# Ninety-nine shared exponential pairs, VectorE's lists taken by turns, and the last skip products on VectorE, in a kernel that mixes an SSM and an attention block

## Chip, core and metric

The kernel runs on one core of one Trainium2 chip. The metric is the device time of one execution in microseconds. Engines are called PE (matrix products), ACT (ScalarE), DVE (VectorE), POOL (GpSimd) and SP (SyncE, which here issues nearly all DMAs).

## What is computed

With x of 2048 tokens by 1024 channels (bf16), a gate g per token mixes an SSM a and an attention block b:

```python
g = sigmoid((x * gate_w).sum(-1))
h[t] = Lam_bar * h[t-1] + B_bar @ x[t]            # 1024 complex states
a = 2 * Re(C @ h) + x * Dskip
b = softmax(q k^T / sqrt(32)) v @ wo              # 32 heads of 32, q k v = x @ wqkv
out = g * a + (1 - g) * b
```

## The kernel before

**Attention in bursts.** The 32 heads are taken in 8 groups of 4 (`GROUPS`), the queries in 8 blocks of 256 (`QUNITS`), the keys in 8 blocks of 256 (`BURSTS`): 512 bursts. `burst` (from L1612) issues eight score products (L1624) into PSUM and two exponentials on ACT of 128x1024 each (L1643). `pv` (L1709) multiplies their results with V, some bursts later. After eight bursts `normalize` (L1716) takes a reciprocal and a product on DVE from PSUM's bank "O", and a transposing DMA brings the result to OT.

**Shared exponentials.** In some bursts ACT's second exponential leaves out a quarter and is 128x768 (L1640). DVE does that quarter: it copies 256 columns from PSUM to integers (`x_in`, L1633), before ACT may take the rest; two such bursts make a *pair*, on which DVE runs three polynomial steps over 512 columns (`x_q`, L1667, L1668, L1664, each reading the one before), POOL makes bf16 bits of them (L1665), and PE multiplies them with V (L1688). `X_PLAN` lists the pairs, 92 of them; `X_AT` says which bursts of eight they take. A group of four bursts in the plan holds one pair.

**Dense work between.** Each burst has room for four products of 512 columns (`MM_PER_PERIOD`), all accumulating in PSUM bank 7: chains of eight or sixteen products, whose evacuation DVE does at their end. The chains are: u = B x (`d_u`, L1457, 64 chains, 32 items with real and imaginary part), projections to Q, K and V of the next group (`d_qk` L1426, `d_v` L1445), SSM output (`d_c`, L1504, 32 tiles of 128x512 in four quarters `ch` of the sequence, each tile sixteen products in four bursts), and output products (`d_out`, L1535). A tile of SSM output also has four products of 128 columns with a diagonal matrix of Dskip (`diagD`, L1510): that is D times x. Its evacuation (L1517) multiplies by g into the single buffer `Ag`, and a DMA stores it (`ag_scratch`); the store is read back for the output products (`ld_a`, L1527).

**SSM items.** Each u goes out to DRAM and comes back by `ld_u` (L1474) into one buffer. An item's steps on DVE (`item_ops`, L1353 and the scans L1362) form the states of 512 tokens. SSM output of a quarter needs all eight items of it.

**Order.** `build` writes the order of every engine's queue by hand, burst by burst. DVE has three lists: `xbg` (steps of pairs), `bg` (steps of items) and `bg2` (tables, folding of C, and the like). At the end of each burst the planner has room up to a limit, tries how many steps of each list fit by a table of durations, and takes the best sum; steps of one list follow each other, those of pairs first. A chain's evacuation follows at its end. SP's queue is in program order: weights are loaded at the 26th and 29th burst of a group, C by `ld_c` (L1081) from burst 28 on, two transposes each four bursts, B by `ld_b` (L1076) after each evacuation of u. K and V weights have two buffers. The output weights come in five loads.

**Tail** (from L1956). Sums of the last output tiles, split into a high and a low bf16 part (`hi`, `lo`, L1553 and L1554), are put into PSUM by four products with the identity (`preload`, L1975) ahead of the last value products.

Of the kernel before, what the change touches and what calls it, by code (L numbers as in the profile page):

```python
# [922 lines left out]
GROUPS = 8  # L923
# [9 lines left out]
C_LOADS = 28  # L933

X_AT = ((0, 2), (4, 6), (0, 4))
X_PLAN = (64, 72, 80, 88, 92, 96, 100, 104, 108, 112, 116, 120, 124, 128, 132, 136, 144, 152, 160, 168, 172, 176, 180, 184, 188, 192, 200, 208, 216, 224, 228, 232, 236, 240, 244, 248, 252, 256, 260, 264, 272, 280, 288, 296, 304, 312, 316, 320, 324, 328, 332, 336, 344, 352, 356, 360, 364, 368, 372, 376, 380, 384, 388, 392, 396, 400, 404, 408, 412, 416, 420, 424, 428, 432, 436, 440, 444, 448, 452, 456, 460, 464, 468, 472, 476, 480, 484, 488, 492, 496, 500, 504)
X_COLS = 256
F_TS, F_ST = 1.32, 1.24
I_MM = 0.61
X_LAST = 0.735  # L940
# [18 lines left out]
class FastPath:  # L959

    def __init__(self, nc, S, es, d, flag):
# [11 lines left out]
        wb = T("wb", [128, 8192], BF)  # L973
        self.wq = wb[:, 0:1024].rearrange("p (a n) -> p a n", a=8)
        self.wkv = wb[:, 1024:5120].rearrange("p (s q a n) -> p s q a n", s=2, q=2, a=8)
        self.bT = wb[:, 5120:8192].rearrange("p (s a n) -> p s a n", s=3, a=8)

        row = lambda o, n: wb[:, o:o + 1024 * n].rearrange("p (a n) -> p a n", a=n)
        self.wo3 = [row(1024, 2), row(5120, 3), row(3072, 1), self.cT[0][:, 0:1, :], self.cT[0][:, 1:2, :]]
        self.wo = [(self.wo3[0][:, a, :], "wo0") for a in range(2)] + [(self.wo3[4][:, 0, :], "wo4")] + [(self.wo3[1][:, a, :], "wo1") for a in range(3)]  # L980
        self.wo += [(self.wo3[3][:, 0, :], "wo3"), (self.wo3[2][:, 0, :], "wo2")]
# [5 lines left out]
        self.hpx = wb[:, 5120:8192].rearrange("p (k n) -> p k n", k=6)  # L987
# [18 lines left out]
        self.diagD = T("diagD", [128, 8, 128], BF)  # L1006
        self.init = T("init", [128, 2, 8], F32)
# [57 lines left out]
    def w_of(self, g, part):  # L1065
        return (self.wkv[:, g % 2, part - 1], ("w", g % 2, part)) if part else (self.wq, ("w", 0, 0))
# [241 lines left out]

    def fold_ops(self, j):
# [32 lines left out]
    def item_ops(self, j, ch, n):  # L1342
# [9 lines left out]
        def tt(c, o, a, b, op, r, w):  # L1352
            ops.append((c, lambda: dve(lambda e: e.tensor_tensor(o, a, b, op), r, w)))  # L1353
# [3 lines left out]
        ops.append((0.0, lambda: self.used_u(n)))  # L1357
# [6 lines left out]
        if ch < 3:  # L1364
            ops.append((0.0, lambda: self.pool(lambda e: e.tensor_copy(self.hl[:, :, j], ht[:, :, 511]), [("ht", 0), ("ht", 1)], [("hl", j)])))
# [770 lines left out]
```

## Time and profile before

| What | Value |
|---|---|
| Runs of before | 929.36 us median of 3 (927.99 to 930.2) |
| The profiled execution | 928.11 us, of which the span on the core is 926.3 |
| PE, ACT, DVE, POOL busy | 902.5, 907.3, 758.4, 86.8 us |
| Granted PE clock, mean | 0.996 |

How to read it: a line of groups names the source line, the engine, the operation, what it writes and reads, and a count; then busy time, mean duration and idle time before. A line of the chain has start, duration and what ran; the chain is followed back from the last instruction, so what it holds set the end. A line of the timeline has start, duration and, in square brackets, idle time before it and what ended it. An answer by source line gives the shortest, median and longest duration in ns and first and last start in us. Instructions of ACT and PE overlap their neighbours, so starts, not durations, give the pace. DMAs show as their issue on SP's queue (SPq).

### The profile page before, as it was taken

How to read it: one execution, taken by the hardware profiler on the slowest of the kernel's cores; microseconds unless marked ns; L12 is line 12 of the kernel's file. 1: busy time of each engine (PE TensorE's matmuls, PEld its weight loads, DVE VectorE, ACT ScalarE, POOL GpSimd, SP SyncE). 2: the span in 40 equal slices, each digit the busy share in tenths (PEclk: the TensorE clock that was granted, in tenths of full speed). 3: DMA queues.
4: the chain of work that ended last, by engine and by line, in shares of the span. 5: the costliest groups of instructions: out<-in, count | busy, mean ns of one | idle time of the engine just before them, and what ended most of it. 6: DMA issues, size and time to landing. Idle time of an engine off the chain costs nothing.

```text
span 926.3 us, 33979 instructions
## 1 busy us (share of the span) xinstructions
PE 902.5 (97%) x15316; PEld 503.9 (54%) x15316; DVE 758.4 (82%) x1310; ACT 907.3 (98%) x1034; POOL 86.8 (9%) x156
## 2 busy tenths in 40 slices
PE   8899999999999999999999999999999999999996
PEld 4554754557555565546655565555655655445553
DVE  2788989998989999989989999899988655776665
ACT  6999999999999999999999999999999999999996
POOL 2000000111000101011111020000010010001010
PEclk9999999999999999999999999999999999999998
DMA  9569747750457101272012511413001112424312
GB/s 195 87 116 184 93 84 138 144 116 5 81 113 152 50 20 49 67 147 53 19 51 65 126 45 31 104 63 103 20 15 43 31 51 77 156 83 128 114 62 75
DMA packets 170934, 77.69 MB, mean 84 GB/s; under 512 B 147232, under 2 KB 155424, under 8 KB 170784
## 3 DMA queue, kind: packets, MB, share of 16 engines
q1 hardware_dynamic: 168624, 74.94, 36.3%
q8 instruction: 121, 1.98, 0.9%
q10 hardware_dynamic: 2160, 0.53, 0.3%
q14 instruction: 29, 0.24, 0.1%
HBM read 25.18 MB, written 20.97 MB: 50 GB/s over the span
## 4 chain that ended last, share of the span: by engine, by line
PE 52%; ACT 40%; DVE 4%; DMA 2%; SPq 1%; issue 1%; POOL 0%; DVEq 0%; ACTq 0%
ACT f_pt L1643 32%; PE f_ps L1709 14%; PE f_ps L1624 10%; PE f_ps L1426 9%; PE f_ps L1504 7%; PE f_ps L1457 6%; ACT f_pt L1640 5%; PE f_ps L1445 5%; SPq L1062 1%; ACT f_cT L1643 1%; PE f_ps L1688 1%; DMA f_xT<-in_A_x_dram 1%; ACT f_Et L1643 1%; DMA f_wb<-in_A_B_im_dram 1%; DMA f_ub<-u_scratch 0%
## 5 line engine op out<-in xcount | busy, mean ns | idle before, releaser
L1643 ACT ACTIVATE f_pt<-f_ps 128x1024 bf16<-128x1024 f32 x760 | 728.8, 1090 | 1.5 <-PE f_ps L1624 1.3
L1709 PEld LDWEIGHTS f_ps<-f_V,f_pt 128*128 128x128 bf16 x7184 | 222.2, 96 | 95.3 <-issue 68.7
L1709 PE MATMUL f_ps<-f_V,f_pt 128*128 128x33 bf16 x7184 | 258.0, 178 | 0.0
L1624 PE MATMUL f_ps<-f_Q,f_K 32*128 32x256 bf16 x4096 | 203.3, 273 | 10.8 <-ACT f_pt L1643 3.3
L1640 ACT ACTIVATE f_pt<-f_ps 128x768 bf16<-128x768 f32 x184 | 165.3, 898 | 0.7 <-PE f_ps L1624 0.6
L1624 PEld LDWEIGHTS f_ps<-f_Q,f_K 32*128 32x128 bf16 x4096 | 60.7, 92 | 148.0 <-ACT f_pt L1643 120.6
L1457 PE MATMUL f_ps<-f_xT,f_wb 128*128 128x512 bf16 x512 | 131.5, 379 | 1.6 <-DMA f_wb<-in_A_B_im_dram 0.7
L1665 POOL TENSOR_SCALAR f_xp<-f_xq 128x512 int16<-128x512 f32 x92 | 67.3, 732 | 646.0 <-DVE f_xq L1664 471.3
L1426 PE MATMUL f_ps<-f_xT,f_wb 128*128 128x512 bf16 x464 | 119.3, 379 | 0.1
L1633 DVE TENSOR_SCALAR f_xi<-f_ps 128x256 int32<-128x256 f32 x184 | 77.4, 421 | 17.6 <-PE f_ps L1624 13.3
L1362 DVE TENSOR_TENSOR_SCAN f_ht<-f_pf,f_init,f_ut 128x512 bf16<-128x512 f32 x64 | 81.3, 1279 | 0.0
L1504 PE MATMUL f_ps<-f_cT,f_hp 128*128 128x512 bf16 x272 | 74.5, 379 | 0.1
L1667 DVE SCALAR_TENSOR_TENSOR f_xq<-f_xi 128x512 f32<-128x512 uint16 x92 | 63.7, 692 | 3.2
L1668 DVE SCALAR_TENSOR_TENSOR f_xq<-f_xq,f_xi 128x512 f32<-128x512 f32 x92 | 63.6, 692 | 3.1
L1664 DVE SCALAR_TENSOR_TENSOR f_xq<-f_xi,f_xq 128x512 f32<-128x512 int16 x92 | 63.5, 690 | 2.6
L1457 PEld LDWEIGHTS f_ps<-f_xT,f_wb 128*128 128x128 bf16 x512 | 40.1, 96 | 40.5 <-issue 8.6
L1535 PE MATMUL f_ps<-f_wb,f_OT 128*128 128x512 bf16 x188 | 61.2, 381 | 0.4 <-DVE f_Et L1547 0.4
L1445 PE MATMUL f_ps<-f_wb,f_xT 128*128 128x128 bf16 x896 | 59.3, 219 | 0.0
L1426 PEld LDWEIGHTS f_ps<-f_xT,f_wb 128*128 128x128 bf16 x464 | 36.1, 96 | 35.6 <-issue 7.6
L1461 DVE CAST f_ub<-f_ps 128x512 bf16<-128x512 f32 x64 | 44.1, 688 | 10.4 <-PE f_ps L1457 9.7
L1445 PEld LDWEIGHTS f_ps<-f_wb,f_xT 128*128 128x128 bf16 x896 | 50.4, 97 | 3.8 <-issue 3.8
L1722 DVE RECIPROCAL f_rc<-f_ps 128x8 f32<-128x8 f32 x63 | 13.1, 207 | 47.6 <-PE f_ps L1688 43.5
(149 smaller groups left out, 822.5 us busy)
## 6 DMA issues: line engine op xcount, KB each, us to landing
u_scratch<-f_ub SPq DMA_DIRECT2D x64, 128.0 KB, 2.1
f_ub<-u_scratch SPq DMA_DIRECT2D x32, 256.0 KB, 3.0
ag_scratch<-f_Ag SPq DMA_DIRECT2D x32, 256.0 KB, 2.0
f_hp<-ag_scratch SPq DMA_DIRECT2D x32, 256.0 KB, 3.0
f_wb<-in_B_wqkv_dram SPq DMA_DIRECT2D x21, 256.0 KB, 4.1
out_dram<-f_xT SPq DMA_DIRECT2D x16, 256.0 KB, 2.2
f_OT<-f_On SPq DMA_TRANSPOSE x63, 2.3
f_wb<-in_B_wo_dram SPq DMA_DIRECT2D x1, 768.0 KB
```

Source lines behind the costliest of these rows:

```text
L1362: ops.append((1.24, lambda ri=ri: dve(lambda e: e.tensor_tensor_scan(ht[:, ri, :], rr, ut[:, ri, :], self.init[:, ri, j:j + 1], ALU.mult, ...
L1426: mms.append((1, lambda e, f, l, a=a, w=w: e.matmul(ps[:, bank, :], w[:, a, :], xT[:, a, 512 * ch:512 * (ch + 1)], start=f, stop=l), [tok] ...
L1445: m = e.matmul(ps[:, bank, 128 * q:128 * (q + 1)], xT[:, a, 128 * kt:128 * (kt + 1)], w[:, a, :], start=(a == 0), stop=(a == 7))
L1457: mms.append((1, lambda e, f, l, a=a: e.matmul(ps[:, 7, :], bT[:, (2 * n + ri) % 3, a, :], xT[:, a, 512 * ch:512 * (ch + 1)], start=f, sto ...
L1504: mms.append((1, lambda e, f, l, j=j, ri=ri, h=h: e.matmul(ps[:, 7, :], h[:, cols], cT[ri][:, j, 512 * cb:512 * (cb + 1)], start=f, stop=l ...
L1624: m = e.matmul(ps[:, 2 * sl[h // 2] + h % 2, 256 * kl:256 * (kl + 1)], K[32 * h:32 * h + 32, g % 2, 128 * kt:128 * (kt + 1)], Q[32 * h:32 ...
L1633: first = self.dve(lambda e: e.tensor_scalar(self.xi[:, b % 2, X_COLS * n:X_COLS * (n + 1)], ps[:, 2 * s + 1, 512 - X_COLS:512], X_A, X_LO ...
L1640: self.S.op("act", lambda e: e.activation(flat(self.tile[p]), flat(ps[:, 2 * s:2 * s + 2, :]), ACT.Exp, scale=SCALE), reads=[("S", s)], wr ...
L1643: self.act(lambda e: e.activation(self.tile[p], ps[:, 2 * s:2 * s + 2, :], ACT.Exp, scale=SCALE), [("S", s)], [("pt", p)], "exp")
L1665: self.pool(lambda e: e.tensor_scalar(bits, xq[:], X_K, 128.0 * (E0 + 126.0), ALU.mult, ALU.add), ["xq"], p2, "x_p")
L1667: return [(0.73, 0.0, lambda: self.dve(lambda e: e.scalar_tensor_tensor(xq[:], lo, E2 / E3 * w, lo, ALU.add, ALU.mult), i2, ["xq"], "x_q") ...
L1709: m = e.matmul(ps[:, 6, o:o + 33], self.tile[p][:, h2, 256 * kl + 128 * qt:256 * kl + 128 * (qt + 1)], V[:, g % 2, 2 * i + kl, h, :], star ...
```

## The change

1. **Seven more pairs**: 268, 276, 284, 292, 300, 308 and 348 are new in `X_PLAN`, 99 in all.
2. **Steps by turns**: each step now carries a duration and a surcharge `DEP` if the step before it came from the same list; `mixed` adds up a choice of steps from the three lists, changing list at every step where it can, and says from which list comes the first. Durations in the table are smaller by 0.01 to 0.12 us.
3. **D times x**: in the last quarter (`ch` 3, eight tiles, 32 bursts) the diagonal products go; x and a broadcast Dskip are loaded, DVE writes x times g times D into `Ag` (`skip`, put on `bg2`), and the evacuation adds PSUM times g to it.
4. **Loads**: K, V and Q weights have one buffer each; K and V are loaded at the first burst of a group for the next (the first time K at the 18th, V at the start), Q at the 39th. C's loads begin at burst 32. All output weights but the last load when SSM output is done.
5. **hi and lo** go on `bg2`; **preload** is split, two products ahead of the last value products and two behind.

```diff
-C_LOADS = 28
+C_LOADS = 32
+W_AT = (38, 0, 17)
-I_MM = 0.61
-X_LAST = 0.735
+DEP = 0.12
+I_MM = 0.6
+X_LAST = 0.615
...
+    def ld_skip(self, dn):
+        tt, cb = divmod(dn.tile, 2)
+        self.dma(lambda e: e.dma_start(self.xn[:, dn.k], self.x2[128 * tt:128 * (tt + 1), 512 * cb:512 * (cb + 1)]), [], [("xn", dn.k)], "ld_xn")
+
+    def skip(self, dn):
+        tt, cb = divmod(dn.tile, 2)
+        if not dn.skipped:
+            dn.skipped = True
+            self.dve(lambda e: e.scalar_tensor_tensor(self.Ag, self.xn[:, dn.k], self.gcol[:, 0, tt:tt + 1], self.Dbc[:, 512 * cb:512 * (cb + 1)], ALU.mult, ALU.mult),
+                     [("xn", dn.k), "Dbc", "g0"], ["Ag"], "skip")
...
-        for q in range(4):
+        for q in range(4 if ch < 3 else 0):
...
+                self.skip(dn)
+                self.dve(lambda e: e.scalar_tensor_tensor(a, ps[:, 7, :], self.gcol[:, 0, tt:tt + 1], a, ALU.mult, ALU.add), [("bank", 7), "g0"], [at], "evac_c")
...
-                    self.dve(lambda e: e.tensor_copy(hi, su), [("sum7", i)], [("hi", i)])
-                    self.dve(lambda e: e.tensor_tensor(lo, su, hi, ALU.subtract), [("sum7", i), ("hi", i)], [("lo", i)])
+                    self.bg2 += [(0.34, lambda: self.dve(lambda e: e.tensor_copy(hi, su), [("sum7", i)], [("hi", i)])),
+                                 (0.72, lambda: self.dve(lambda e: e.tensor_tensor(lo, su, hi, ALU.subtract), [("sum7", i), ("hi", i)], [("lo", i)]))]
...
+    def mixed(self, xs, bs, ts):
+        rest = {"x": list(xs), "b": list(bs), "t": list(ts)}
+        t, lane, lead = 0.0, self.lane, ""
+        while True:
+            some = [s for s in "xbt" if rest[s]]
+            if not some:
+                return t, lead
+            s = next((s for s in some if s != lane), some[0])
+            if rest["b"] and rest["b"][0][0] == 0.0:
+                s = "b"
+            c, d = rest[s].pop(0)
+            lead = lead or s
+            if c > 0:
+                t += c + (d if s == lane else 0.0)
+                lane = s
...
-            if pg == 25 and g + 2 < GROUPS:
-                assert g or not (proj[0] or cur and cur.tag == "proj")
-                for part in (1, 2):
-                    self.ld_w(g + 2, part)
-            if pg == 28 and g + 1 < GROUPS:
-                assert not (cur and cur.tag == "proj")
+            if pg == W_AT[1 if g else 2] and g + 1 < GROUPS:
+                self.ld_w(g + 1, 1)
+                if g:
+                    self.ld_w(g + 1, 2)
+            if pg == W_AT[0] and g + 1 < GROUPS:
+                assert not proj[0]
                 self.ld_w(g + 1, 0)
...
+                            if ch == 3:
+                                self.bg2.append((0.73, lambda dn=cur: self.skip(dn)))
+                            if cs and cs[0][0] == 3:
+                                if ch == 2:
+                                    self.dma(lambda e: e.dma_start(self.Dbc[:], self.d["A_Dskip"].unsqueeze(0).to_broadcast([128, 1024])), [], ["Dbc"], "ld_D")
+                                self.later.append((p + 2, lambda dn=cs[0][1]: self.ld_skip(dn)))
...
-                            v = (u + (0.3 * i if ended is not None else 9.0 * i) + 0.05 * sum(bs[:j]), i, j, k)
+                            v = (u + (0.3 * i if ended is not None else 9.0 * i) + 0.05 * sum(x[0] for x in bs[:j]), i, j, k, lead)
...
-        preload()
-        self.pv(4 * NBURST - 4, 4 * NBURST)
+        preload(0)
+        self.pv(4 * NBURST - 4, 4 * NBURST - 2)
+        self.pv(4 * NBURST - 2, 4 * NBURST)
+        preload(1)
```

More of the change, by code (lines that the diff above doesn't have):

```diff
@@ L1520, in evac @@
             self.c_end = self.p
-        return self.chain(mms, "c", evac)
+        dn = self.chain(mms, "c", evac)
+        dn.tile, dn.k, dn.skipped = tile, k % 2, False
+        return dn
     def ld_a(self, k):
@@ L1744, in build @@
             self.ld_b(m)
-        for part in (1, 2):
-            self.ld_w(1, part)
+        self.ld_w(1, 2)
         self.plan()
@@ L1784, in build @@
         first = FIRST
-        wo1 = wo6 = last = False
+        wo1 = last = False
         nal = nc = 0
@@ L1806, in build @@
                 if n == 1:
-                    self.xbg += [[c, wait, f] for c, wait, f in self.x_ops(b)]
+                    self.xbg += self.x_ops(b)
+                self.lane = "x"
             q0, q1 = self.quarters[p]
@@ L1838, in build @@
+            if pg == W_AT[0] and g + 1 < GROUPS:
+                assert not proj[0]
                 self.ld_w(g + 1, 0)
             wsv = self.d["B_wo"].rearrange("(a p) n -> p a n", p=128)
[L1840 to L1842 removed]
+            if not wo1 and not cs and cur is None and self.c_left[3] == 0:
```

140 lines of the change are left out of this document (71 added, 69 removed).

## The prediction

> **What bounds the kernel now.** I began with the page's first part, then asked for ScalarE's two exponentials by source line, then for the chain of work in a quiet stretch, and last for PE's timeline at a few bursts.
>
> ```profile
> PE 902.5 (97%) x15316; PEld 503.9 (54%) x15316; DVE 758.4 (82%) x1310; ACT 907.3 (98%) x1034; POOL 86.8 (9%) x156
> ...
> L1643 ACT ACTIVATE f_pt<-f_ps x760: 1018/1103/1309, 9.9 to 916.1; 128x1024 bf16<-128x1024 f32 x190
> L1640 ACT ACTIVATE f_pt<-f_ps x184: 805/908/978, 131.9 to 907.2; 128x768 bf16<-128x768 f32 x184
> ...
> 491.47 6.42 ACT f_pt L1643 x7
> 497.90 0.70 ACT f_pt L1640
> ...
> 910.69 6.60 ACT L1643 ACTIVATE f_pt<-f_ps 128x1024 bf16<-128x1024 f32 x7
> ```
>
> Two engines look full, so busy shares decide nothing. The chain does: seven full exponentials take 6.42 us, 0.917 each, and a shortened one 0.70. The recorded durations (1.10 and 0.91) are longer because neighbours overlap. The program has 512 bursts with two exponentials each: 1024, of which 184 are short. 840 x 0.917 + 184 x 0.70 = 899 us. The first starts at 9.9 (the fourth number of L1643's row) and the last ends at 910.69 + 6.60 = 917.3: 907.4 us. So ScalarE is the bound nearly everywhere, some 8 us are stalls of it, and 9 us of the span lie behind it.
>
> PE is close behind. The next rows are the first score products of bursts 264, 284, 356, 380, 402 and 434, so that differences give the pace.
>
> ```profile
> 482.09 0.29 PE L1624 MATMUL f_ps<-f_Q,f_K 32*128 32x256 bf16 x4
> 517.55 0.40 PE L1624 MATMUL f_ps<-f_Q,f_K 32*128 32x256 bf16 x8
> 644.50 0.29 PE L1624 MATMUL f_ps<-f_Q,f_K 32*128 32x256 bf16 x4
> 685.83 0.40 PE L1624 MATMUL f_ps<-f_Q,f_K 32*128 32x256 bf16 x8
> 723.93 0.40 PE L1624 MATMUL f_ps<-f_Q,f_K 32*128 32x256 bf16 x8
> 780.24 0.40 PE L1624 MATMUL f_ps<-f_Q,f_K 32*128 32x256 bf16 x8
> ```
>
> Bursts 356 to 379 run projections beside two pairs per eight bursts: 41.33 / 24 = 1.722 us each, which is ScalarE's own pace (12 x 0.917 + 4 x 0.70 = 13.80 per eight, 1.726 each). Bursts 402 to 433 also have two pairs, but run SSM output with its diagonal products: 56.31 / 32 = 1.760. There PE is the bound by 0.034. Bursts 264 to 283 run SSM output with one pair per eight: 1.773, where ScalarE needs 14.24 / 8 = 1.780.
>
> **The change, part by part.**
>
> *Seven more pairs* (of bursts 268, 276, 284, 292, 300, 308, 348). A pair shortens two exponentials by 0.217: 0.43 us, 3.0 for seven. That is only taken where PE doesn't become the bound. 268, 276 and 348 lie in SSM output with diagonal products, if its place stays: eight bursts go from 14.24 to 8 x 1.760 = 14.08, 0.16 each. 284 is half in it: 0.30. The other three take 0.43. Sum: **-2.1 us** (-3.0 if PE never binds).
>
> *Diagonal products*, four in each of the last quarter's eight tiles:
>
> ```profile
> 501.28 0.22 PE L1510 MATMUL f_ps<-f_diagD,f_xT 128*128 128x128 bf16 x1
> 501.34 0.38 PE L1504 MATMUL f_ps<-f_cT,f_OT 128*128 128x512 bf16 x1
> ```
>
> The next product starts 0.06 us behind one, so 32 are 1.9 us of PE, one per burst. ScalarE's 1.726 stops the gain: (1.760 - 1.726) x 32 = **-1.1 us**. What replaces them is VectorE's, with room there:
>
> ```profile
> 480.00:640.00 160.00, 159.02 (x2684) 87.92 (x2682) 146.70 (x236) 160.00 (x183) 18.07 (x27) 1.00 0.30 76
> 724.00:780.00 56.00, 56.00 (x928) 30.06 (x928) 31.35 (x56) 55.87 (x65) 4.94 (x8) 1.00 0.14 44
> ```
>
> The columns behind the window are PE, weight load, VectorE, ScalarE, GpSimd. VectorE is busy 31.35 of 56 us there; eight skip steps of 128x512 add 8 x 0.7 (the rows of f_xq below have that size). The evacuation still reads PSUM, with one operand more; this form isn't shown alone, and I leave it at its 0.75 (row at 744.85 below), since up to 0.3 more would still end in that idle time. The nine loads for it, with DMA engines busy 0.14 of that stretch (the column before the last), I cost at nothing; the price without cover is the rival below.
>
> *Steps by turns.* Does VectorE have time for seven pairs between 480 and 640 us? It idles 13.3 of 160.
>
> ```profile
> 504.31 0.69 DVE L1667 SCALAR_TENSOR_TENSOR f_xq<-f_xi 128x512 f32<-128x512 uint16 x1
> 505.03 0.69 DVE L1668 SCALAR_TENSOR_TENSOR f_xq<-f_xq,f_xi 128x512 f32<-128x512 f32 x1
> 505.76 0.69 DVE L1664 SCALAR_TENSOR_TENSOR f_xq<-f_xi,f_xq 128x512 f32<-128x512 int16 x1
> 506.37 1.70 DVE L1353 TENSOR_TENSOR f_ut<-f_ht,f_tq 128x512 f32<-128x512 bf16 x2
> ...
> L1667 DVE SCALAR_TENSOR_TENSOR f_xq<-f_xi x62: 691/692/693, 138.7 to 697.2; 128x512 f32<-128x512 uint16 x62
> ```
>
> A step that reads its predecessor's result starts 0.72 to 0.73 us behind it (504.31, 505.03, 505.76); one that doesn't starts after 0.61 (506.37). So a stranger between two such steps saves 0.11. A pair costs 2 x 0.42 (the copies from PSUM, row at 745.59 below) + 3 x 0.72 = 3.0 us now, seven cost 21. Saving: 62 pairs up to 700 us with three places each, 62 x 3 x 0.11 = 20 us, and the SSM items have dependent steps as well; bounds 0 and about 30. I take the middle, 15 us, since a stranger isn't always ready. With the idle time that covers the seven pairs. So the turns bring no time themselves; they pay for the pairs.
>
> The Trainium skill (VectorE: DVE Perf Modes, section "The DRAIN you can't avoid") states that the next operation starts only when the pipe is empty, whether or not a semaphore lies between, and that chained operations can't skip it. By that rule order would be worth nothing here; the 0.61 and 0.72 above don't bear it out for operations without a dependence.
>
> *Moved loads.* ScalarE's largest stall stands at burst 34:
>
> ```profile
> 66.79 1.30 SPq L1081 DMA_TRANSPOSE f_cT<-in_A_C_im_dram  x1
> 68.14 1.28 SPq L1071 DMA_DIRECT2D f_wb<-in_B_wqkv_dram  x1
> ...
> 69.53 3.79 DMA f_ub<-u_scratch
> ...
> 75.27 0.57 PE L1709 MATMUL f_ps<-f_V,f_OT 128*128 128x33 bf16 x16 [1.24 <-DVE f_On L1723]
> ...
> 77.36 1.94 ACT L1643 ACTIVATE f_OT<-f_ps 128x1024 bf16<-128x1024 f32 x2 [1.34 <-PE f_ps L1624]
> ```
>
> The load of u is issued at 69.53, behind two transposes of C and a weight load (3 x 1.3, some 3.9 us of SP's queue), lands at 73.3, VectorE waits for it with the normalization behind, PE waits for that, ScalarE for PE. The change starts the C loads at burst 32 and that weight load at 38, so u goes 3.9 us earlier: **-1.3 us** (bounds -1.4 and 0, if the next collision takes its place). Four bursts later, C is still not late: the last loads slip some 7 us, and the first step on C waits until tables are made.
>
> ```profile
> L1318 DVE TENSOR_SCALAR f_OT<-f_cT,f_pf x8: 1275/1282/1287, 135.9 to 288.8; 128x2048 f32<-128x2048 bf16 x8
> L1081 SPq DMA_TRANSPOSE f_cT<-in_A_C_im_dram x8: 1242/1299/2480, 66.8 to 115.6; - x8
> ...
> 404.64 4.86 DMA f_wb<-in_A_B_im_dram
> ...
> 401.95 1.88 SPq L1071 DMA_DIRECT2D f_wb<-in_B_wqkv_dram  x2
> ...
> 410.97 2.85 ACT L1643 ACTIVATE f_pt<-f_ps 128x1024 bf16<-128x1024 f32 x3 [0.33 <-PE f_ps L1624]
> ```
>
> At 402 the same happens to a load of B behind two weight loads: 0.4 us with its start. It goes: **-0.4**. But K and V weights now load at each group's first burst, where in three groups B and u stream as well; one such stall in three: **+0.4** (0 to 1.2). The output weights now load in one bunch; the eight bursts of Q projections between the last SSM tile and the first output product (14 us) hide them.
>
> *The split into hi and lo* is now placed by the planner instead of run at once:
>
> ```profile
> 815.13 0.44 DVE f_Et L1553
> ...
> 823.94 0.35 DVE f_xi L1633
> ...
> 820.07 0.84 ACT L1640 ACTIVATE f_pt<-f_ps 128x768 bf16<-128x768 f32 x1
> ...
> 824.36 0.81 ACT L1640 ACTIVATE f_pt<-f_ps 128x768 bf16<-128x768 f32 x1 [0.57 <-PE f_ps L1624]
> ```
>
> Short to short normally takes 3 x 0.917 + 0.70 = 3.45 us; here 4.29, since the copy from PSUM for the shared exponential queues behind the split. **-0.9** (0 to -1.2).
>
> *Tail.* Four preload products stand ahead of the last value products:
>
> ```profile
> 916.34 1.71 PE f_ps L1975 x4
> 918.04 0.45 PE f_ps L1709 x16
> ```
>
> The last exponential ends at 917.3, but the chain has the last value products only from 918.04. Two of four preloads moved behind (0.85 us) let them follow the exponential at once: between 0 and -0.7, I take **-0.6**.
>
> **Sum.** -2.1 - 1.1 - 1.3 - 0.4 + 0.4 - 0.9 - 0.6 = -6.0 us. The profiled execution took 928.11 (span 926.3 and 1.8 around it); it is 1.25 below the median of the runs shown, 929.36. I forecast against the median: 929.4 - 6.0 = **923.4 us**. Chance **0.55**.
>
> **The rivals.**
>
> *PE never binds and all stalls go* (chance 0.08): pairs -3.0, diagonal -1.1, stalls -1.4, -0.4 and -1.2, tail -0.7, nothing new: -7.8, 921.6.
>
> *Stalls only move* (0.20). Against: the two queue stalls have loads named ahead of them that leave. For: B, u and weights still share one queue. Pairs, diagonal and tail remain, -3.8: 925.6.
>
> *The turns free nothing* (0.10): the change does not do what it says. Then VectorE is 21 us short against 13 idle, SSM items end about 8 to 10 us later, the last quarter's tiles with them, and the output products, which fill PE to the end, run over by about 5 us: 923.4 + 5 = 928.4. The 0.61 beside the 0.72 speaks against it; that a stranger must be ready in the same burst speaks for it. The Trainium skill's rule on the DRAIN, named above, would lead here.
>
> *The skip step waits for the store* (0.07), on the slow side:
>
> ```profile
> ag_scratch<-f_Ag SPq DMA_DIRECT2D x32, 256.0 KB, 2.0
> ...
> 744.85 0.75 DVE L1517 TENSOR_SCALAR f_Ag<-f_ps,f_gcol 128x512 f32<-128x512 f32 x1 [2.29 <-PE f_ps L1504]
> 745.59 0.42 DVE L1633 TENSOR_SCALAR f_xi<-f_ps 128x256 int32<-128x256 f32 x1
> ```
>
> Skip writes the one buffer Ag, which the store of the tile before still reads: free at 745.6 + 2.0 = 747.6, while VectorE could start it at 746.0. Queued behind it are the steps of the pair and the next copy from PSUM. With tiles beginning on even bursts, as now, that copy is due only at 749 and hides the wait. If a gap in PE's work makes tiles begin on odd bursts, it is due at about 747.3, and starts 1.0 to 1.6 us late behind wait and step; ScalarE waits as long, eight times: +8 to +13, 931.5 to 936. It decides from the first tile of the last quarter: even or odd.
>
> **Range and chances.** The first three cases hold 0.83; bounds of the unknown terms widen them: 919.5 to 928.5. A measurement of this kernel tells about 0.2% (1.9 us) from no change. Faster: the first three, 0.83. Same: the turns that free nothing, 0.10. Slower: 0.07.
>
> **What would show it.** L1643 falls by 14, its short form rises to 198; bursts of the last quarter's SSM output at 1.726; those around 264 to 283 at 1.76, not below; f_xq steps starting 0.61 behind strangers; no ACT idle near 77 and 824; preload split in the tail. I am wrong if VectorE's copies from PSUM come late between 480 and 640 us, if the skip steps show idle time ended by a store, or if ScalarE waits behind group starts.

## The result, and the profile after

The changed kernel took **927.05 us**, median of 11 runs (926.28 to 928.83); the kernel before took 930.2, median of 11 (927.94 to 934.19). Ratio 0.9965, interval 0.995 to 0.998: faster by some 3.1 us, about half of the forecast 6.0. The profiled execution took 927.15, with a span of 925.3.

First the page's busy line, then ScalarE's two exponentials by source line (count; shortest, median and longest duration in ns; first and last start):

```profile
PE 899.5 (97%) x15284; PEld 499.8 (54%) x15284; DVE 775.3 (84%) x1353; ACT 905.1 (98%) x1034; POOL 86.3 (9%) x163
```
```profile
L1663 ACT ACTIVATE f_pt<-f_ps x746: 1017/1102/1231, 9.9 to 915.3; 128x1024 bf16<-128x1024 f32 x187
L1660 ACT ACTIVATE f_pt<-f_ps x198: 804/906/974, 131.6 to 906.3; 128x768 bf16<-128x768 f32 x198
```

198 short exponentials are there, and 826 full ones (746 and 80 into other buffers). They need 826 x 0.917 + 198 x 0.70 = 896.0 us, 3.0 less than before. VectorE is 17 us busier.

What led to the answer was no view of its own but a **table by stage**: from ScalarE's records, the time from the first exponential of one burst to that of another. Each column is one profiled execution (us). "Before, second" is the kernel before, profiled once more (below).

| Bursts | before | before, second | after | C at 32 alone | second Ag buffer | 92 pairs, turns |
|---|---|---|---|---|---|---|
| start to burst 0 | 9.92 | 10.13 | 9.90 | 10.17 | 9.89 | 9.85 |
| 0 to 64 | 121.07 | 122.97 | 120.78 | 119.87 | 120.50 | 120.30 |
| 64 to 256 | 337.07 | 336.74 | 337.43 | 336.59 | 337.42 | 337.44 |
| 256 to 402 (all new pairs) | 256.50 | 256.52 | 255.96 | 256.51 | 255.80 | 257.02 |
| 402 to 434 (last SSM output) | 56.29 | 56.29 | 57.05 | 56.29 | 55.20 | 56.52 |
| 434 to the last exponential | 136.43 | 136.43 | 135.31 | 136.44 | 135.31 | 135.31 |
| behind it, to the span's end | 9.02 | 9.22 | 8.90 | 8.96 | 8.28 | 8.43 |
| the execution | 928.11 | 930.03 | 927.15 | 926.55 | 924.13 | 926.62 |

Apart from waits for DMAs, a stage whose order wasn't touched repeats to 0.1 us (56.29 three times), so differences of 0.3 can be read here, where medians don't tell apart what differs by less than some 1.5. Three things stand out. The stage of the new pairs gained 0.5 rather than some 2. The last SSM output **lost** 0.8 rather than gaining 1.1. And the stage with the stall at burst 34 is not always 121.07: the first profile of before had caught a good execution.

**The stall at burst 34 is gone**: SP's queue and ScalarE in the timeline of after. The load of u (L1488) is issued at 65.70 and no exponential near 77 shows idle time in brackets:

```profile
64.32 1.24 SPq L1079 DMA_TRANSPOSE f_wb<-in_A_B_re_dram  x1
65.70 0.48 SPq L1488 DMA_DIRECT2D f_ub<-u_scratch  x1
67.37 0.32 SPq L1476 DMA_DIRECT2D u_scratch<-f_ub  x1
...
74.51 1.94 ACT L1663 ACTIVATE f_pt<-f_ps 128x1024 bf16<-128x1024 f32 x2
76.44 1.94 ACT L1663 ACTIVATE f_OT<-f_ps 128x1024 bf16<-128x1024 f32 x2
```

**The turns work.** In the timeline of VectorE the last step of a pair (L1684) starts 0.94 behind the middle one with a stranger between; the stranger starts 0.61 behind the middle step and the last one 0.33 behind the stranger:

```profile
507.92 0.69 DVE L1688 SCALAR_TENSOR_TENSOR f_xq<-f_xq,f_xi 128x512 f32<-128x512 f32 x1
508.53 0.42 DVE L1367 TENSOR_TENSOR f_hp<-f_tq,f_ut 128x512 bf16<-128x512 bf16 x1
508.86 0.68 DVE L1684 SCALAR_TENSOR_TENSOR f_xq<-f_xi,f_xq 128x512 f32<-128x512 int16 x1
```

**A kind of stall that before had once, and smaller**, here at burst 185 (bursts 289, 329 and 385 have the same): the timeline of VectorE, GpSimd, PE and ScalarE.

```profile
341.33 0.41 DVE L1653 TENSOR_SCALAR f_xi<-f_ps 128x256 int32<-128x256 f32 x1
341.66 0.68 DVE L1367 TENSOR_TENSOR f_tq<-f_ht,f_Et 128x1024 bf16<-128x1024 bf16 x1
342.26 0.69 DVE L1684 SCALAR_TENSOR_TENSOR f_xq<-f_xi,f_xq 128x512 f32<-128x512 int16 x1
...
343.03 0.62 POOL L1685 TENSOR_SCALAR f_xp<-f_xq 128x512 int16<-128x512 f32 x1 [1.95 <-DVE f_xq L1684]
...
343.70 0.27 PE L1726 MATMUL f_ps<-f_V,f_xp 128*128 128x33 bf16 x4 [0.56 <-POOL f_xp L1685]
...
345.22 1.02 ACT L1663 ACTIVATE f_pt<-f_ps 128x1024 bf16<-128x1024 f32 x1 [0.30 <-PE f_ps L1644]
```

The pair's last step comes behind a scan, an evacuation and a product of another list, GpSimd's conversion follows it, PE has the value products (L1726) next in its order and stands 0.56 for them, and the score products queued behind are late for ScalarE. Such stalls cost 0.6 to 0.8 us each. The rows of the waits, before (L1688) and after (total us, times, longest):

```profile
PE f_ps L1688 <- POOL f_xp L1665: 0.3, 1, 0.3
```
```profile
PE f_ps L1726 <- POOL f_xp L1685: 2.0, 4, 0.6
```

**The skip step waits for the store.** The timeline around the worst of six (SP, VectorE, ScalarE), then the row of the waits for all of them (total us, times, longest):

```profile
765.33 1.18 SPq L1767 DMA_TRANSPOSE f_OT<-f_On  x1
766.56 1.61 SPq L1536 DMA_DIRECT2D ag_scratch<-f_Ag  x1
...
770.05 0.75 DVE L1320 SCALAR_TENSOR_TENSOR f_Ag<-f_xn,f_gcol,f_Dbc 128x512 f32<-128x512 bf16 x1 [2.01 <-DMA ag_scratch<-f_Ag]
770.72 0.68 DVE L1684 SCALAR_TENSOR_TENSOR f_xq<-f_xi,f_xq 128x512 f32<-128x512 int16 x1
771.32 0.42 DVE L1653 TENSOR_SCALAR f_xi<-f_ps 128x256 int32<-128x256 f32 x1
771.77 0.81 ACT L1660 ACTIVATE f_pt<-f_ps 128x768 bf16<-128x768 f32 x1 [1.13 <-DVE f_xi L1653]
```
```profile
DVE f_Ag L1320 <- DMA ag_scratch<-f_Ag: 4.9, 6, 2.0
```

The evacuation starts at 765.50 and ends at 766.25. Its store stands behind a transpose of the normalization on SP's queue, is issued at 766.56 and lands 3.39 us later, where 2.0 had been the median before; VectorE waits at the skip step until 770.05, with the pair's step and the copy from PSUM behind it, and ScalarE waits 1.13 for that copy.

**hi and lo** no longer delay a copy: no idle time at 820 and 823, and short to short is 823.46 - 820.00 = 3.46, the normal 3.45.

```profile
820.00 0.92 ACT L1660 ACTIVATE f_pt<-f_ps 128x768 bf16<-128x768 f32 x1
820.73 2.95 ACT L1663 ACTIVATE f_pt<-f_ps 128x1024 bf16<-128x1024 f32 x3
823.46 0.92 ACT L1660 ACTIVATE f_pt<-f_ps 128x768 bf16<-128x768 f32 x1
```

**Tail.** The chain of work of after; the last value products follow the last exponential at once:

```profile
907.26 9.18 ACT f_pt L1663 x10
916.44 0.05 issue
916.48 0.38 PE f_ps L1747 x8
```

### The profile page after: what moved, and what is told of

Read it like the earlier page. It is cut to its first block, busy times and chain, and to the rows that moved or that the text cites. A ratio compares the mean times of both kernels' runs of the same rounds, so it can differ in the third digit from the quotient of the medians.

```text
span 925.3 us, 33993 instructions
## 1 busy us (share of the span) xinstructions
PE 899.5 (97%) x15284; PEld 499.8 (54%) x15284; DVE 775.3 (84%) x1353; ACT 905.1 (98%) x1034; POOL 86.3 (9%) x163
## 4 chain that ended last, share of the span: by engine, by line
PE 53%; ACT 37%; DVE 5%; DMA 1%; issue 1%; SPq 1%; POOL 0%; DVEq 0%
ACT f_pt L1663 29%; PE f_ps L1747 14%; PE f_ps L1644 10%; PE f_ps L1440 9%; PE f_ps L1518 7%; PE f_ps L1471 6%; ACT f_pt L1660 6%; PE f_ps L1459 5%; ACT f_cT L1663 1%; SPq L1065 1%; ACT f_Et L1663 1%; DVE f_ht L1376 1%; PE f_ps L1726 1%; DMA f_xT<-in_A_x_dram 1%; DMA ag_scratch<-f_Ag 1%
## 5 line engine op out<-in xcount | busy, mean ns | idle before, releaser
L1663 ACT ACTIVATE f_pt<-f_ps 128x1024 bf16<-128x1024 f32 x746 | 718.7, 1088 | 2.6 <-PE f_ps L1644 2.3
L1660 ACT ACTIVATE f_pt<-f_ps 128x768 bf16<-128x768 f32 x198 | 176.8, 893 | 1.5 <-DVE f_xi L1653 1.5
L1653 DVE TENSOR_SCALAR f_xi<-f_ps 128x256 int32<-128x256 f32 x198 | 83.4, 421 | 11.5 <-PE f_ps L1644 7.1
L1688 DVE SCALAR_TENSOR_TENSOR f_xq<-f_xq,f_xi 128x512 f32<-128x512 f32 x99 | 68.5, 692 | 3.3
L1687 DVE SCALAR_TENSOR_TENSOR f_xq<-f_xi 128x512 f32<-128x512 uint16 x99 | 68.5, 692 | 3.3
L1684 DVE SCALAR_TENSOR_TENSOR f_xq<-f_xi,f_xq 128x512 f32<-128x512 int16 x99 | 68.1, 688 | 1.9
L1555 PE MATMUL f_ps<-f_cT,f_OT 128*128 128x512 bf16 x156 | 44.7, 378 | 0.0
```

The lines of the kernel that those rows point to most:

```text
L1653: first = self.dve(lambda e: e.tensor_scalar(self.xi[:, b % 2, X_COLS * n:X_COLS * (n + 1)], ps[:, 2 * s + 1, 512 - X_COLS:512], X_A, X_LO ...
L1660: self.S.op("act", lambda e: e.activation(flat(self.tile[p]), flat(ps[:, 2 * s:2 * s + 2, :]), ACT.Exp, scale=SCALE), reads=[("S", s)], wr ...
L1663: self.act(lambda e: e.activation(self.tile[p], ps[:, 2 * s:2 * s + 2, :], ACT.Exp, scale=SCALE), [("S", s)], [("pt", p)], "exp")
L1687: return [(0.61, DEP, lambda: self.dve(lambda e: e.scalar_tensor_tensor(xq[:], lo, E2 / E3 * w, lo, ALU.add, ALU.mult), i2, ["xq"], "x_q") ...
L1688: (0.61, DEP, lambda: self.dve(lambda e: e.scalar_tensor_tensor(xq[:], xq[:], E1 / E3 * w * w, lo, ALU.add, ALU.mult), ["xq"] + i2, ["xq"] ...
```

## The experiments

**Both kernels once more.** The kernel before under a new label, and the one after:

> The kernel before once more, for a second profile. Its median lies 1 to 2 us above the profiled execution, the changed kernel's does not. Theory A: the stalls at bursts 34, 222, 257 and 456 to 459 (1.4, 0.4, 0.6 and 1.2 us) stand in its order and return at the same bursts; what varies from run to run is how long a late load lands, at 34 and 222 above all. Rival: the stalls at 34 and 222 are chance and are missing here.

> The changed kernel once more. Its profile has 3.0 us less of exponentials on ScalarE than before, but 2.3 us more of stalls between them: at bursts 185, 289, 329 and 385 (0.6 to 0.8 us each, 2.7 together), at 421 and 429 (1.8 together), and at 28, 40 and 58 (1.0 together). Theory A: these stalls are written into the order of VectorE's queue, so the same bursts stall again and the median is 927.0 +- 0.5. Rival B: they are chance (DMA traffic), so other bursts stall and the sum differs.

Measured: before 929.85 (927.48 to 931.92), ratio 1.0 (0.9984 to 1.0016); after 926.93 (926.45 to 928.73), ratio 0.9971 (0.9956 to 0.9986). The second profile of before (timeline of ScalarE, then its chain of work) shows where before varies. Below the chain are rows of PE's weight load and of PE, then the windows view from 77 to 80 us of this profile and of the first one (the number behind the five engines is the granted clock):

```profile
79.22 1.94 ACT L1643 ACTIVATE f_OT<-f_ps 128x1024 bf16<-128x1024 f32 x2 [3.04 <-PE f_ps L1624]
```
```profile
69.48 4.35 DMA f_ub<-u_scratch
```
```profile
76.73 0.13 PEld L1457 LDWEIGHTS f_ps<-f_xT,f_wb 128*128 128x128 bf16 x2 [0.38 <-DMA f_wb<-in_A_B_im_dram]
77.14 1.49 PE L1457 MATMUL f_ps<-f_xT,f_wb 128*128 128x512 bf16 x3 [0.68 <-DVE f_ut L1353]
```
```profile
77.00:80.00 3.00, 2.86 (x32) 1.14 (x32) 2.20 (x2) 0.78 (x1) 0.00 (x0) 0.50 1.01 216
```
```profile
77.00:80.00 3.00, 3.00 (x62) 1.69 (x61) 2.86 (x4) 2.64 (x3) 0.00 (x0) 1.00 0.96 209
```

The stall at burst 34 is 3.04 us here and was 1.34 in the first profile, though the load of u was issued at the same time. It explains the 1.9 between the two executions: 122.97 - 121.07 in the table. Three things add up: u landed 0.5 later, B (issued at 70.51) landed 6.18 after its issue in place of 3.81 and held PE's next products, and PE then ran at half its clock, three of these products taking 1.49 us (0.81 at full clock, row 77.23 further below). The half clock is some 0.9 of the stall, an estimate: from these products to ScalarE's next exponential it takes 2.08 us here, and 1.19 in another profile of the same stall at full clock (77.23 to 78.42, further below). The small stall at 411 us is absent: it had been chance. In the second profile of after the same bursts stall as in its first (185, 289, 329, 385, 420 and 428 among them): those stalls lie in the order.

**92 pairs, with the turns and without.** The plan of before in the kernel after; then also `mixed` taking always the first list:

```diff
-X_PLAN = (64, 72, ..., 264, 268, 272, 276, 280, 284, ..., 504)
+X_PLAN = (64, 72, ..., 264, 272, 280, ..., 504)
...
-            s = next((s for s in some if s != lane), some[0])
+            s = some[0]
```

> The changed kernel with the 92 pairs of before; seven pairs less. ScalarE needs 3.0 us more. Theory A (pairs are worth their exponentials, and the late value products come from turns, not from the number of pairs): the four stalls stay, 926.9 + 2.1 to 3.0 = 929.0 to 929.9. Rival C (late value products because VectorE is full with seven more pairs): the stalls go as well, 2.7 less, about 927, so the seven pairs bring nothing net.

> The changed kernel with 92 pairs and without turns: steps of pairs first, then items, then the rest, as before, with the surcharge paid. Theory A: a pair's last step is never displaced, the stalls at the first burst of eight go: 2.7 less than with turns and 92 pairs, about 926.5, level with the changed kernel. Rival C: no difference to turns with 92 pairs beyond 0.5 us.

Measured: 926.93 (926.17 to 927.98), ratio 0.997 (0.9953 to 0.9986), and 926.63 (926.02 to 927.92), ratio 0.9969 (0.9955 to 0.9982). Against after's 926.93 and 927.05 seven pairs and the turns are worth nothing that medians show; the first expectation's 929 or more fell. By the table the pairs are worth 257.02 - 255.96 = 1.06 in their stage against the same kernel without them, of 3.04 that ScalarE's work shrank by; against before only 0.54. PE's timeline with 92 pairs says what the 257.02 holds:

```profile
592.11 0.81 PE L1471 MATMUL f_ps<-f_xT,f_wb 128*128 128x512 bf16 x3 [0.56 <-DMA f_wb<-in_A_B_im_dram]
...
681.31 0.27 PE L1726 MATMUL f_ps<-f_V,f_xp 128*128 128x33 bf16 x4 [0.50 <-POOL f_xp L1685]
```

The first is a load of B that came late at burst 326 (about 0.4 for ScalarE), which after just escapes; without it the pairs are worth about 0.7. The second is a late value product at burst 377. That at 185 is there too, but those at 289, 329 and 385 are not: these three come with the seven pairs. Without turns late value products remain, at bursts 105, 185 and 377, at 0.3 to 0.5 each. (With 99 pairs and no turns the planner's order ends with output chains left over. So in the planner's sums the turns do pay for the pairs.)

**The pair's steps first** at the start of each eight bursts, if the planner has room for one:

```diff
+                if best[1] and p % 8 == 0:
+                    lead = "x"
```

> In each eighth burst, the last before a pair's value products, the planner takes the pair's steps first; else all as in the changed kernel. Theory A: turns put a step of another list ahead of a pair's last step, GpSimd's conversion comes too late, PE waits 0.56 us for it and ScalarE for PE; without it the four stalls at 185, 289, 329 and 385 go: -2.7 us, 924.3. Rival C: VectorE is simply full there, so the step displaced comes late in its turn and delays an evacuation instead: within 0.5 us of 927.0.

Measured: 926.05 (924.95 to 928.24), ratio 0.9965 (0.9953 to 0.9977): 0.9 under after on the same chip, between the two expectations. The four stalls became smaller, not nothing. VectorE, GpSimd and PE in its timeline:

```profile
340.88 0.68 DVE L1684 SCALAR_TENSOR_TENSOR f_xq<-f_xi,f_xq 128x512 f32<-128x512 int16 x1
341.49 0.68 DVE L1367 TENSOR_TENSOR f_tq<-f_ht,f_Et 128x1024 bf16<-128x1024 bf16 x1
...
341.65 0.99 POOL L1685 TENSOR_SCALAR f_xp<-f_xq 128x512 int16<-128x512 f32 x1 [1.34 <-DVE f_xq L1684]
...
342.70 0.27 PE L1726 MATMUL f_ps<-f_V,f_xp 128*128 128x33 bf16 x4 [0.33 <-POOL f_xp L1685]
```

The last step now goes ahead of the product, so GpSimd starts 0.6 earlier relative to the copy before it; but its conversion runs beside that product and takes 0.99 instead of 0.62. Of 0.6 won, 0.37 is lost, and PE still waits 0.33.

**A second buffer for skip.** Odd tiles use the memory of `diagD`, which the last quarter no longer reads:

```diff
+        self.Ag2 = self.diagD[:].rearrange("p j n -> p (j n)").bitcast(F32)
-            self.dve(lambda e: e.scalar_tensor_tensor(self.Ag, ...
+            self.dve(lambda e: e.scalar_tensor_tensor(self.Ag2 if dn.k else self.Ag, ...
-        a = self.Ag
-        at = "Ag"
+        a, at = (self.Ag2, "Ag2") if ch == 3 and k % 2 else (self.Ag, "Ag")
```

> Of the last quarter's SSM tiles every other one gets a second buffer for skip, evacuation and store, in the room of the diagonal matrices, which are no longer read then. Theory A: the skip step's waits for the store (4.9 us in six waits) go, and the two stalls of ScalarE at bursts 421 and 429 with them: -1.8 us against the changed kernel, 925.2. Rival B: VectorE has idle time there and the stalls come from elsewhere: no change, 927.0.

Measured: 925.38 (924.13 to 925.97), ratio 0.9955 (0.9938 to 0.9971), 1.55 under after on the same chip. The 32 bursts take 55.20 us, 1.09 less than before and 1.85 less than after. At the place where after waited 2.01 us, its timeline of VectorE has no idle time:

```profile
766.27 0.69 DVE L1688 SCALAR_TENSOR_TENSOR f_xq<-f_xq,f_xi 128x512 f32<-128x512 f32 x1
766.88 0.74 DVE L1321 SCALAR_TENSOR_TENSOR f_Ag<-f_xn,f_gcol,f_Dbc 128x512 f32<-128x512 bf16 x1
```

**The diagonal products back.** The kernel after, with PE's diagonal products in the last quarter too and no skip step or load:

```diff
-        for q in range(4 if ch < 3 else 0):
+        for q in range(4):
...
-            if ch < 3:
+            if ch < 4:
...
-                            if ch == 3:
+                            if ch == 4:
-                            if cs and cs[0][0] == 3:
+                            if cs and cs[0][0] == 4:
```

> The kernel after, with the diagonal products back in the last quarter of SSM output and without the skip steps and their loads; the rest as after. Theory (the waits of the skip step on the store of Ag ate the gain): the 32 bursts of the last quarter go back to PE's pace of about 1.760 us each, +1.1, and the two stalls behind waiting skip steps (0.5 + 1.24 in after) go, -1.7. Sum -0.6: about 926.3 where after has 926.9, against a before of 929.5 (ratio 0.9965). In the trace: no VectorE idle time ended by the store ag_scratch with ScalarE idle behind it; bursts 402 to 433 at 1.76. Rival (as predicted, the skip step cost nothing): +1.1, 928.0, ratio 0.998.

Measured: 926.28 (924.76 to 928.34), ratio 0.9963 (0.9945 to 0.9981). The windows view from 724 to 780 us of after, of this kernel and of the one with two buffers (busy us of PE, weight load, VectorE, ScalarE and GpSimd):

```profile
724.00:780.00 56.00, 54.14 (x885) 26.79 (x882) 35.53 (x64) 54.46 (x64) 4.94 (x8) 1.00 0.20 61
```
```profile
724.00:780.00 56.00, 56.00 (x932) 30.12 (x930) 31.16 (x56) 55.87 (x65) 4.94 (x8) 1.00 0.14 44
```
```profile
724.00:780.00 56.00, 55.82 (x913) 27.96 (x910) 36.80 (x66) 56.00 (x66) 4.94 (x8) 1.00 0.21 62
```

PE busy throughout (the products back), ScalarE idle 1.54 us (after: the waits), ScalarE busy throughout (two buffers). So D times x on VectorE is worth the 1.1 forecast, if it has a buffer of its own; as made it costs 0.76 (57.05 against 56.29).

**hi, lo and preload alone**, in the kernel before (the two edits of the change's part 5):

> The kernel before, with only two parts of the change: hi and lo on the list bg2, and the preload split, two products behind the last value products. Theory (these terms were sized about right, 0.9 to 1.1 and 0.6 to 0.8): -1.5 to -1.9, so 927.6 to 928.0 against a before of 929.5, ratio 0.9982; in the trace no ScalarE idle near bursts 456 to 459, and the last value products follow the last exponential at once. Rival (the stalls only move): within 0.5 of before, ratio above 0.9995; in the trace another copy from PSUM late in the same stretch.

Measured: 928.25 (925.77 to 930.71) against 929.65, ratio 0.998 (0.996 to 1.0001): right in size, at the edge of what can be told. In the trace the last stage goes from 136.43 to 135.3. The same trace has a stall of 1.2 at burst 94, where B lands 5.5 us after its issue; no other trace has it, so that is chance.

**C's loads.** First the kernel after with C at burst 28 again; then the kernel before with C at 32 and nothing else:

```diff
-C_LOADS = 32
+C_LOADS = 28
```

> The kernel after with the loads of C starting at burst 28 again (C_LOADS = 28), so that two transposes stand ahead of the load of u at burst 32 on SP's queue, but no weight load. Theory (the queue of three loads, 3.9 us, made the stall at burst 34, and each of the three counts): u is issued about 2.6 us later than in after (68.3 instead of 65.7) and ScalarE idles 0.3 to 2 us around 75 to 80 us: 927.3 to 928.9 where after has 926.9. Rival (the weight load alone made the stall, or the load of u now has more room than it needs): no idle time there, 926.9 within 0.3.

> The kernel before with one constant changed: the loads of C start at burst 32 (C_LOADS = 32). VectorE's order is the same as before, the weight load stays. Theory of the prediction (SP's queue made the stall at burst 34): the load of u is issued some 2.6 us earlier, at about 66.9, lands by 71, VectorE's first step on it doesn't wait, and the 1.45 to 3.15 us of ScalarE's idle time there go: 926.6 to 928.1 where before has 929.6, ratio 0.9969 to 0.9984. Rival (the gain of after in that place comes from elsewhere): a stall stays there or comes back within the next ten bursts, ratio above 0.9990.

Measured: 927.36 (925.71 to 928.18), ratio 0.9961 (0.9943 to 0.9979), and **926.63** (925.9 to 928.97) against 930.0, ratio 0.9967 (0.9953 to 0.9981). The median of the first, 0.4 over after's, decides nothing. Its trace has no stall at burst 34 although the load of u is issued at 68.16, so my expectation that each of the three loads counts fell: moving the weight load or moving C is enough. The second says that one constant brings as much as the whole change. There the load of u is issued 2.96 us earlier than in before (66.57 against 69.53) but lands only 1.0 earlier, at 72.3. So it still isn't quite in time (timeline of VectorE), but VectorE's wait of 0.92 reaches nobody:

```profile
72.30 0.69 DVE L1353 TENSOR_TENSOR f_ht<-f_ub,f_Et 128x1024 bf16<-128x1024 bf16 x1 [0.92 <-DMA f_ub<-u_scratch]
```

**Only the order on VectorE.** In after, and with C at 28 too, VectorE's first step on the late u stands behind the normalization. So perhaps the order was the cause. In the kernel before, with all loads as before, the item is told to be ready two bursts later:

```diff
-        self.u_ready[n] = self.p + U_LAG
+        self.u_ready[n] = self.p + U_LAG + (2 if n == 1 else 0)
```

> The kernel before with all loads as before, and only the first two steps on the late u put behind the normalization and the evacuation on VectorE (one step of C's folding taken ahead of them instead). Theory now (the load alone is not the cause: VectorE's order put a step that waits for it ahead of the normalization, and c_loads_28 had no stall because there the order was another): no ScalarE idle time near 75 to 80 us although u lands at 73 to 74 as before, 1.45 to 3.15 less: 926.6 to 928.1 where before has 929.6. Rival (the late load has to be paid in any order): the stall moves to the next evacuation, ratio above 0.9990.

> The same kernel as item_step_later_on_before, profiled once more: the profile of that run was of its fastest execution (927.32), while eleven of its twelve took 929.3 or more. If the late u is the cause, a slower execution shows ScalarE idle for about 2 us between 70 and 85 us behind a step that waits for u. If it shows none there, the 2 us lie somewhere else, and what the loads of C at burst 28 do to the typical execution is not the wait for u.

Measured: 930.25 (927.32 to 933.28) against 930.0, ratio 1.0012 (0.9997 to 1.0028): nothing gained. Its profiled execution was its fastest (927.32), without a stall; the second profile (928.55) has one (timelines of VectorE, PE and ScalarE, then the chain):

```profile
74.76 0.69 DVE L1461 CAST f_ub<-f_ps 128x512 bf16<-128x512 f32 x1 [1.38 <-DMA u_scratch<-f_ub]
...
77.23 0.81 PE L1457 MATMUL f_ps<-f_xT,f_wb 128*128 128x512 bf16 x3 [2.75 <-DMA f_wb<-in_A_B_im_dram]
...
78.42 1.94 ACT L1643 ACTIVATE f_OT<-f_ps 128x1024 bf16<-128x1024 f32 x2 [2.55 <-PE f_ps L1624]
```
```profile
70.53 6.43 DMA f_wb<-in_A_B_im_dram
```

The step on u no longer stands in the way, yet the evacuation waits for the store of u, and PE's next products wait for B: both were issued behind the load of u on the same queue, at 70.05 and 70.53. My theory of the order falls. The queue is the cause, and it holds three transfers that are needed within some 5 us, not one. B lands 6.43 us after its issue here (3.78 in the profile without a stall); with it the stall is 2.55 even when u is out of the way.

**The small parts together**: before with hi and lo on bg2, the split preload and C at 32; no new pair, no turns, diagonal products as they were.

> The kernel before with hi and lo on bg2, the preload split, and C_LOADS = 32: no new pair, no turns, diagonal products as before. Theory (pairs, turns and D times x bring nothing on net, and the rest of the change brings all of it): -1.4 (the run with hi, lo and preload alone) and -1.5 to -3.1 (burst 34): 925.1 to 926.7 where before has 929.6, as fast as after or faster. Rival (pairs or D times x bring some 2 us of their own): 927.5 or more, clearly behind after's 926.9.

Measured: **926.2** (924.42 to 928.35), ratio 0.9958 (0.9943 to 0.9973), no slower than the whole change. Pairs, turns and D times x, as made, bring nothing on net.

**A better version.** After with the second buffer, and the pair's steps first only at four places, for two bursts each; then without burst 327:

```diff
+                if best[1] and p in (184,183, 288,287, 328,327, 384,383):
+                    lead = "x"
```

> The second buffer for skip, and a pair's steps first only in bursts 183, 184, 287, 288, 327, 328, 383 and 384, ahead of the four late value products. Before, with the steps first in each eighth burst, GpSimd's conversion began 0.6 us earlier but took 1.00 in place of 0.62 us, beside VectorE's bf16 product, so half the gain was lost. Theory A: begun two steps earlier it is done in time wherever VectorE is: the four stalls go, and the skip waits: 926.9 - 2.7 - 1.7 = 922.5. Rival C: the displaced scan or product makes an evacuation late instead: above 924.

> The kernel after with a second buffer for skip (odd tiles write into the memory of the diagonal matrices, which is free in the last quarter) and with the pair's steps first at bursts 183, 184, 287, 288, 328, 383 and 384 only (not at 327, where the variant with four places for two bursts each got a new stall of 0.36 + 0.48 at burst 326). Theory (that stall was made by the order at 327): it goes, 0.8 less than the 924.0 of that variant: about 923.2, ratio 0.993. Rival (VectorE is full there and whatever goes first makes something else late): 924.0 or more, with a stall of 0.6 back at burst 328 or 329.

Measured: **924.02** (923.22 to 925.04), ratio 0.9936 (0.9913 to 0.9959), and 924.42 (923.2 to 927.62), ratio 0.994 (0.9916 to 0.9964). The expected 922.5 and 923.2 were missed. The first had a stall at burst 326 (timelines of PE's weight load and of ScalarE):

```profile
590.62 0.56 PEld L1472 LDWEIGHTS f_ps<-f_xT,f_wb 128*128 128x128 bf16 x4 [0.97 <-DMA f_wb<-in_A_B_im_dram]
590.87 0.81 ACT L1660 ACTIVATE f_pt<-f_ps 128x768 bf16<-128x768 f32 x1 [0.25 <-DVE f_xi L1653]
592.06 2.85 ACT L1663 ACTIVATE f_pt<-f_ps 128x1024 bf16<-128x1024 f32 x3 [0.38 <-PE f_ps L1644]
```

The second hasn't (its bursts 256 to 402 take 255.24 against 256.20), and its profiled execution took 923.71 against 925.04, but the medians don't tell the two apart. The order at burst 327 isn't the cause, as I had it: the two kernels differ only from that burst on, and the stall lies ahead of it. PE waits there for B, which stands on SP's queue behind B's other half, K and V weights, a load of u, a transpose of the normalization and a store, a collision that the prediction had named; B landed 11.4 us after the start of burst 320 in the first kernel and 10.5 in the second and in after. So this difference is chance. The four late value products are smaller and still there in both (PE waits 0.26 to 0.34), with a conversion of 1.00 us ahead of them (at 594.09 in the second). Both kernels are some 5.4 us faster than before and faster than after.

One more variant had the second buffer, the pair's steps first in each eighth burst and a normalization costed 0.26 us later in the first 60 bursts. It was expected at 921.5, with a rival of 925 or more, and took 924.31 (923.6 to 926.91), but its output is off by 2.0%, for a reason not known, so nothing is built on its time.

## Why the prediction came out as it did

The direction, the bound and the range held: ScalarE's exponentials still set the time, from 9.9 to 916.4 us. That the range held is partly luck: one term lost where it should have gained, and another gained more than its bound allowed. The predicted 923.4 missed, by these steps:

**Seven more pairs, -2.1: this step failed.** The pairs and the turns made their stage 0.54 shorter. By eight bursts at a time, of the 3.04 that ScalarE saved 0.9 went to PE's pace in SSM output, about as predicted (1.77 and 1.74 a burst at bursts 264 to 279, where I had 1.76 and not below), and 2.0 to a wait that I had not priced: the value products of a pair, late at bursts 289, 329 and 385. (0.4 came back, as the one late pair of before, at burst 257, is gone.) I counted VectorE's *time* for seven pairs and found it. But as VectorE fills, the last step of a pair comes behind a scan, an evacuation and another list's product; PE takes its work in a fixed order and stands for it. With 92 pairs the three stalls are gone; the one at burst 185 stays, so it comes from the new order. I had named late copies from PSUM as the sign of being wrong; it was the step behind them.

**Diagonal products, -1.1: the gain was right, "costed at nothing" was wrong.** With a buffer of its own the stage gains 1.09. As made it loses 0.76. The rival had the mechanism and the wrong point of decision. Tiles did begin on even bursts, where I let the copy at the next burst hide the wait. I had the store free the buffer 2.0 us behind the evacuation's end; at 766.25 (765.50 + 0.75) it took 3.7, to 769.95: 0.3 until its issue, behind the normalization's transpose on SP's queue, and 3.4 from there to its landing, which is most of the difference. Six waits of up to 2.01 come of it, two of which reach ScalarE. So not eight times 1.0 to 1.6, as the rival had it, but it did take the whole gain.

**Moved loads, -1.3 - 0.4 + 0.4: the mechanism was right and the size was off.** The stage with burst 34 lost 2.2 us against the typical execution of before. C at 32 alone gives 122.97 - 119.87 = 3.1, of which the half clock is some 0.9. I sized it from one execution, in which B landed 3.8 us after its issue, and put -1.4 as the outer bound, although the stall was made by a queue whose landing times vary. The stall at 411 us was chance. The new collision of weight loads (+0.4) doesn't show in the two profiles of after, but it was sized about rightly: at burst 326 PE waits for B, 0.38 to 0.56 us in three other traces of the new loads (92 pairs with and without turns, C at 28), and its weight load 0.97 in a fourth (four places). Unforeseen were three small stalls in after, 0.3 each, at bursts 28, 40 and 58, where the planner puts an item's step between the normalization and an evacuation; that is most of the difference between 120.78 and 119.87.

**hi and lo, -0.9**: 1.12 by the table. **Tail, -0.6**: the last value products do follow the last exponential at once, but what lies behind the last exponential fell only from 9.0 or 9.2 to 8.9, -0.1 to -0.3 (over all traces it is 9.0 to 9.2 without the split and 8.2 to 9.1 with it).

**Sum by the table**, against the second profile of before: start -0.2, bursts 0 to 64 -2.2, 64 to 256 +0.7 (one of the late pairs is there, at burst 185), the pairs -0.6, last SSM output +0.8, last stage -1.1, tail -0.3: -3.0 before rounding. The medians say -3.1. So the gain came from one moved load and one moved pair of steps.

The rival "stalls only move" (925.6) came nearest in spirit, but with the wrong members: the old stalls went, and the new ones grew where VectorE was filled. What stays open: why B's landing at burst 34 varies between 3.8 and 6.4 us (and u's between 3.8 and 4.4) from one execution to the next, and what halves the granted clock in that stall in one profile and not in another; no run here tells which of the transfers ahead slows them.

## What to carry to other kernels

When an engine that feeds others is filled up, ask not only whether its time suffices but which of its results has a consumer with a fixed order behind it: that one comes late first. A buffer that a store reads is free when the store has landed, and the store's place on its queue belongs in that sum. And a stall behind a DMA queue is sized from several executions: list every transfer behind the culprit and who needs it within its landing time, for clearing the first only shows the next.

## What the runs showed of the hardware

GpSimd's conversion of 128x512 takes 0.62 us by itself and beside copies, casts and steps that VectorE began later. Begun 0.16 us behind a VectorE product of two operands from SBUF it takes 0.99 (341.65 above, and 24 others between 0.99 and 1.0 in the traces of before, after and the kernel with the pair's steps first), and behind a scan of 1.28 us it takes 1.52. So it stands while VectorE's instruction runs, and the pair's last step is best followed on VectorE by a copy or cast from PSUM, beside which it took 0.62 every time. One operand alone isn't enough: behind a 128x2048 step that reads one tile from SBUF it took 1.58, twice. The Trainium skill (SBUF — State Buffer, section "Who interferes with whom") states the rule: a VectorE instruction with two inputs from SBUF and a GpSimd one that reads SBUF exclude each other, and the second waits until the first is done. The trace agrees in kind; in size the 0.37 lost is less than the 0.52 that the product's record still runs.

DMAs of one size differ much in landing: the transposed load of a half of B took 3.81 us from issue to landing in one execution of before and 6.18 in another, at the same place of the queue (3.78 and 6.43 in two of the kernel whose item is ready later).

The granted clock of PE fell to 0.50 for 3.4 us from 76.64 in the second profile of before, among waits of PE at burst 34; behind a wait of 2.75 us at the same place (the kernel whose item is ready later) it stayed at 1.00.
